# A second batch of filler matmuls behind the last y of unit 0, stages and loads at new positions

## The chip, the cores and the metric

One core of one Trainium2 chip runs the whole program in one launch. The metric is the device time of that core in microseconds (us), less is better; the time before is the median of three runs. A further execution was taken by the hardware profiler, and all rows below come from it.

## The reference

The reference has two parts, one behind the other.

```python
# q, k, v, a_re, a_im: (4, 8, 768, 48) float32
mag = sqrt(a_re**2 + a_im**2)
scale = minimum(mag, 0.999) / (mag + 1e-6)
for t in range(768):                      # a complex state S of 48 x 48 per batch and head
    S = (a_re + 1j*a_im)[t][:, None] * scale[t][:, None] * S + k[t] (outer) v[t]
    y[t] = q[t] @ real(S)
x = y.transpose(0, 2, 1, 3).reshape(3072, 384)
# w_in: (384, 2048), w_out: (2048, 384), drawn as float64
h = x @ w_in
g = h * tanh(softplus(h))                 # softplus(h) = h above 20
out = (g @ w_out).astype(float32)
```

## The kernel before, in words

The 3072 rows are cut into 12 units of 256 time steps (three per batch), a unit into two chunks of 128 steps. Each unit goes through three stages.

1. `ew_steps(u)`, elementwise. Loads of a_re and a_im (tiles R and I, L247), q and k (QK, L255) and v (V, L262). ScalarE (ACT) takes squares, logarithms and exponentials (L123); VectorE (DVE) sums the log magnitudes along time (the scan at L333), ACT takes two exponentials of the sum and GpSimd (POOL) multiplies q and k with them (L375, unit 0 on DVE). The angles go the same way: an arctangent on ACT (L143), a second scan (L347), the reduction to one turn (L352, L353), sines on ACT (L143; each way into and out of this group costs a table load, L131), and the products with q and k (`rot`, L397: the X products with t=0 of a unit 1 or 2 chunk on POOL, the others on DVE). DMAs on SyncE's (SP's) queue relay the products into the tile T (L388), in which rows are the 96 inner positions of a head. For units 0 and 1 the chunks are handled one by one, later units in one piece.
2. `attn_steps(u)`, attention by chunks on TensorE (PE). `kn` transposes k (L459, copied by ACT at L460), `amat` takes k times q (pa, L467; masked into am by DVE at L470), `upd` takes the new part of the state (pd, L497) that DVE adds and scales (L501, L503, L505; from unit 1 on L505 is POOL's), `yv` sums y in PSUM (L483), and ACT copies it out (L488). `fin` relays y into the layout of x by four DMAs (xf, L516) and splits it into a high and a low part, xH by ACT (L157) and xL by DVE (L158), three column groups each.
3. `moe_steps`, the two dense layers. `mm1(j)` takes x times the j-th of eight pairs of column groups of w_in, 18 matmuls into ph (L543) in three products (xH·wiH, xL·wiH, xH·wiL); ACT and DVE make g of it (L547 to L553, split into gh and gl at L556); `mm2(j)` multiplies with w_out into po (L571).

The weights come as 64-bit numbers. `convert` makes 12 chunks of w_in (raw) and 12 of w_out (wraw) into a high and a low 32-bit part: ACT turns the low word (L123), DVE shifts the high word (L190, L194), POOL adds the two (L199), then a cast gives wiH or wo (L157, two of three on ACT, one on DVE) and DVE takes the rest (wiL or wo, L158). All of it stands between the start of the program and the last of the first dense layers, beside the elementwise work of units 0 to 3.

The order is set by numbers. Each step has a place in a plan (EW for elementwise, AT for attention, LD for loads, WP for weights, FIN0 for unit 0's `fin`, WK for the filler) and a shift of its rank (ES, TS, WS, MB); `tile_kernel` sorts the steps by place to write them and by shifted place to give them a priority, and a scheduler at build time fixes from priorities and dependencies the order of each engine's instructions. Every engine then runs its list in order, and waits where the head of it waits. SP issues the DMAs in list order too.

The filler is `warm` (L428): 18 matmuls of bf16 with 512 columns into a PSUM tile that nobody reads, which wait by a hand-made dependency for unit 0's first reduced angle (L353).

Of the kernel before, what the change touches and what calls it, by code (L numbers as in the profile page):

```python
# [41 lines left out]
GACT = 0  # L42
GATE = -1
GRP = 2
RG, QG, GN = 5, 1, 0
SQ0, SORD, CGA, CGN, CGD, ACTG = 1, 0, 3, 3, 0, 0
YDVE = []
RQ = [(), ()]
LG, WG = -1, 12
W1 = 0  # L50
ADDV = 12
CLAMPP, MAGP = 0, 0
# [1 line left out]
ROTP = [2]  # L54
TREE = 1
WXB, WRB, WI = 1, 2, 512
FIN0 = -3.39
FS = 0.0
TRUNC = 0
AFTERX = 0  # L60
NUN = 12
SUBP = 0
MULP = 1
LONG = 2
WIDE = 1
NWARM, WREP, WK = 2, 9, -9.4
FAST = [0, 1]
EW = [(-16.31, -10.95), (-12.73, -8.83), (-13.6, -11.78), (-17.21, -10.84), (-16.32, -10.6)]
AT = [(-7.75, -4.28), (-4.18, -0.81), (-7.43, -2.2), (-9.42, -3.06), (-10.26, -2.73)]
WP = [(-7.98, -3.45), (-3.03, 2.5), (2.11, 8.49), (9.4, 9.68)]  # L70
WS = [-3.58, -0.64, -1.09, 0.24]
ES = [2.49, -0.99, -0.86, 1.6]
TS = [-0.14, -1.22, 2.46, -0.05]
MB = [-1.35, -0.11]
WL1 = -1.83
RB = 2
XB = 2
LD = [(-17.86, -16.7, -16.5), (-19.19, -20.26, -20.22), (-17.97, -17.71, -17.6), (-21.41, -14.83, -16.39), (-24.18, -15.85, -17.38)]
WL = 512
XRUNS = ((0, 0, 0, 32), (0, 1, 32, 16), (64, 1, 64, 16), (0, 2, 80, 32))  # L80
LOW, HIGH, FADED = 0.55, 2e6, 1e-17
# [5 lines left out]
def tile_kernel(ctx, tc, q, k, v, are, aim, w_in, w_out, out):  # L87
    nc = tc.nc
# [78 lines left out]
    turned = []  # L167
# [4 lines left out]
    def load_win(half):  # L172
        def f():
            for o in range(0, NJ * DF // 2, WL):
                ins = nc.sync.dma_start(raw_in[half][:, o:o + WL],
                                        w_in[:, half * NJ * DF // 2 + o:half * NJ * DF // 2 + o + WL])
                if half:
                    after(ins, placed[3] if o // WL >= RG else qloads[-1] if QG else relayed[-1])
        return f
# [50 lines left out]
    def ew_steps(u):  # L230
# [45 lines left out]
        def get(g):  # L276
            return (*(flat(st[n], g) for n in ("R", "I", "X1")), *(part(st["X"][:, :, :, a], g) for a in range(2)))
# [26 lines left out]
        def slope(g):  # L304
            R, I, X1, x2, x3 = get(g)
            (nc.gpsimd if 0 < u <= MULP else nc.vector).tensor_tensor(I, I, X1, ALU.mult)
            (nc.gpsimd if 0 < u <= CLAMPP else nc.vector).tensor_scalar(I, I, -1.5, 1.5, ALU.max, ALU.min)
# [129 lines left out]

    def attn_steps(u):
        b, uu = divmod(u, NU)
        st = units[u]  # L440
# [6 lines left out]
        def chunk(c):  # L447
            first = uu == 0 and c == 0
            last = uu == NU - 1 and c == NCH - 1
            cs = slice(c * C, (c + 1) * C)  # L450
# [23 lines left out]
            def yv(g):  # L474
                def f():
                    py = ypsum
                    for i in (2 * g, 2 * g + 1):
                        for n, old in enumerate(((True, False), (False, True))[u < WIDE] if not first else (False,)):
                            for par in range(2):
                                h = 2 * i + par  # L480
                                lhs = d["S"][:, h, :] if old else st["V"][:, c, h * D:(h + 1) * D]
                                rhs = st["T"][c][:, h, 0, :C] if old else d["am", h // 4][:, h % 4, :]
                                nc.tensor.matmul(py[64 * par:64 * par + D, i, :], lhs, rhs,  # L483
                                                 start=n == 0, stop=first or n == 1)
                    if g == 1:
                        if c == 0:
                            st["y"] = at.tile([112, 4, TU], F32, tag="y", name="y", bufs=1)
                        (nc.vector.tensor_copy if u < 1 and c in YDVE else nc.scalar.copy)(st["y"][:, :, cs], py)  # L488
                return f

            def upd():
# [100 lines left out]
    plan = []  # L592

    def place(steps, first, last, shift=0.0):
        n = len(steps)
        for i, f in enumerate(steps):
            x = first + (last - first) * i / max(n - 1, 1)
            plan.append((x, len(plan), f, x + shift))
# [3 lines left out]
    for u in range(NUN):  # L602
        slot = slots.get(u, range(NPAIR * u, NPAIR * (u + 1)))
        t0 = slot[0]
        place(ew_steps(u), t0 + EW[min(u, len(EW) - 1)][0], t0 + EW[min(u, len(EW) - 1)][1], ES[min(u, 3)])
        for n, f in enumerate(units[u]["load"]):
            x = t0 + LD[min(u, len(LD) - 1)][n]
            plan.append((x, len(plan), f, x))
        asteps = attn_steps(u)
        if u == 0:  # L610
            plan.append((FIN0, len(plan), asteps.pop(), FIN0 + FS))
        place(asteps, t0 + AT[min(u, len(AT) - 1)][0], t0 + AT[min(u, len(AT) - 1)][1], TS[min(u, 3)])
        moe = moe_steps(units[u], u * TU, u, u < 2)
        for j in range(NPAIR):
            plan.append((slot[j], len(plan), moe[0][j], slot[j] + MB[0]))
            plan.append((slot[j] + LAG + 0.5, len(plan), moe[1][j], slot[j] + LAG + 0.5 + MB[1]))
    plan.append((-15.9, len(plan), load_win(0)))
    plan.append((WL1, len(plan), load_win(1)))
    if NWARM:
        plan.append((WK, len(plan), warm))  # L620
    n = HALF // WI
    for i, f in enumerate((win, wout)):
        for half in range(2):
            place([f(n * half + m) for m in range(n)], *WP[2 * half + i], WS[2 * half + i])
    rank = {x[:2]: i for i, x in enumerate(sorted(plan, key=lambda x: (x[3] if len(x) > 3 else x[0], x[1])))}
# [22 lines left out]
def general(tc, nc, q, k, v, are, aim, pools, moe_steps, split):  # L648
    io, ew, at, ps, dram = (pools[n] for n in ("io", "ew", "at", "ps", "dram"))
    BJ = B * NJ  # L650
    TS = 8
    xs = dram.tile([B, S, DM], F32, name="xs")
# [14 lines left out]
    kv, t1, t2, t3, t4 = w1[:, 0], w1[:, 1], w2[:, 0], w2[:, 1], w3  # L667
    n = B * TS * D
    m = BJ * TS
    big = at.tile([P, n + 5 * m], F32, tag="T", name="big", bufs=TB)  # L670
    more = at.tile([P, 3 * m + BJ * D], F32, tag="T", name="more", bufs=TB)
    vb = big[:, 0:n].rearrange("p (b t e) -> p b t e", b=B, t=TS)
    cols = [x[:, o + i * m:o + (i + 1) * m].rearrange("p (b j t) -> p b j t", b=B, j=NJ)
            for x, o, cnt in ((big, n, 5), (more, 0, 3)) for i in range(cnt)]
    cq, ck, cr, ci, cm, ca, cb, cc = cols
    qs = more[:, 3 * m:].rearrange("p (a e) -> p a e", e=D)
    ysb = at.tile([H, B, TS, D], F32, tag="T", name="ysb", bufs=TB)
    tt, ts = nc.vector.tensor_tensor, nc.vector.tensor_scalar
# [132 lines left out]
```

## Time and profile before

| | us |
|---|---|
| median of three runs | 655.73 |
| the three runs | 652.61, 655.73, 659.77 |
| the profiled execution's own time | 653.54 |
| its span in the trace | 651.7 |

The span begins with the first instruction of the trace and ends with the last; the 1.8 us around it are the launch. In the profile's rows PE, PEld, DVE, ACT and POOL are TensorE's matmuls and weight loads, VectorE, ScalarE and GpSimd, SPq is the DMA queue of SyncE. A timeline row gives start, length, engine, line, operation, the tiles written and read, and in brackets the idle time before it with what ended it. The granted clock is TensorE's, as a share of 2.4 GHz: 1.00 is the upper of its two levels, 0.50 the lower, 1.2 GHz.

### The profile page before, as it was taken

The page shows a single profiled execution, that of the slowest core. Times are in us where ns is not written, and L with a number is a line of the kernel's source. Part 1 is how long each engine was busy: PE and PEld are TensorE (multiplying, and loading weights), DVE is VectorE, ACT ScalarE, POOL GpSimd, SP SyncE. Part 2 cuts the span into 40 slices and gives each one's busy share as a digit, 9 for nine tenths or more (in the row PEclk, how much of TensorE's full clock was granted, in tenths as well). Part 3 has the DMA queues.
Part 4 walks back from the last instruction along what each step waited for, and adds up shares of the span by engine and source line. Part 5 has one row for each costly group of instructions (what it writes and reads, how often), then busy time and mean ns, then how long its engine had stood idle before and what let it go on. Part 6 is the DMA issues. An engine that isn't in the chain of part 4 may idle for free.

```text
span 651.7 us, 11747 instructions
## 1 busy us (share of the span) xinstructions
PE 581.7 (89%) x4468; PEld 554.5 (85%) x4468; DVE 502.1 (77%) x875; ACT 489.2 (75%) x785; POOL 127.5 (20%) x101
## 2 busy tenths in 40 slices
PE   0686956698689999999999999999999999999996
PEld 0475846598579999999989999999899999999995
DVE  6968989999848869878869868978788796544552
ACT  7857967797757778887988977977888878645661
POOL 2316257435201112002003003003012030000000
PEclk9856888599779999999999999999999999999999
DMA  8765723612840270260460530621711602201000
GB/s 303 219 238 142 245 82 101 190 33 85 210 144 13 87 191 5 89 179 1 117 153 25 143 101 26 183 63 29 192 49 49 171 2 83 64 26 25 1 26 29
DMA packets 58528, 67.05 MB, mean 103 GB/s; under 512 B 4960, under 2 KB 51040, under 8 KB 58464
## 3 DMA queue, kind: packets, MB, share of 16 engines
q1 hardware_dynamic: 58464, 66.23, 35.1%
q8 instruction: 37, 0.61, 0.4%
q14 instruction: 27, 0.22, 0.1%
HBM read 36.96 MB, written 5.51 MB: 65 GB/s over the span
## 4 chain that ended last, share of the span: by engine, by line
PE 38%; DVE 23%; ACT 18%; DMA 7%; issue 7%; SPq 5%; POOL 2%; DVEq 0%; POOLq 0%; ACTq 0%
PE ph L543 14%; PE po L571 13%; ACT e L123 6%; ACT L131 4%; PE pa L467 4%; PE ypsum L483 4%; DVE e L548 3%; DMA R<-a_re 3%; ACT X L123 3%; SPq L388 3%; DVE gl L158 3%; DMA T<-QK 3%; DVE X L347 2%; PE pd L497 2%; DVE R L333 2%
## 5 line engine op out<-in xcount | busy, mean ns | idle before, releaser
L571 PE MATMUL po<-wo,gh 128*128 128x384 f32 x768 | 221.0, 348 | 16.8 <-DVE wo L157 6.0
L543 PE MATMUL ph<-xH,wiH 128*128 128x256 f32 x576 | 169.3, 295 | 10.4 <-ACT xH L157 9.6
L543 PE MATMUL ph<-xL,wiH 128*128 128x256 f32 x576 | 167.3, 291 | 3.1 <-DVE xL L158 3.1
L543 PE MATMUL ph<-xH,wiL 128*128 128x256 f32 x576 | 167.7, 291 | 0.9 <-DVE wiL L158 0.9
L571 PEld LDWEIGHTS po<-wo,gh 128*128 128x128 f32 x768 | 141.6, 190 | 22.5 <-DVE wo L157 6.7
L123 ACT ACTIVATE e<-e 128x512 f32<-128x512 f32 x192 | 119.7, 629 | 50.8 <-DVE e L548 48.9
L571 PE MATMUL po<-wo,gl 128*128 128x384 f32 x384 | 131.3, 342 | 0.0
L543 PEld LDWEIGHTS ph<-xH,wiH 128*128 128x128 f32 x576 | 113.4, 197 | 14.4 <-ACT xH L157 10.4
L543 PEld LDWEIGHTS ph<-xL,wiH 128*128 128x128 f32 x576 | 113.4, 197 | 4.1 <-DVE xL L158 4.1
L543 PEld LDWEIGHTS ph<-xH,wiL 128*128 128x128 f32 x576 | 113.5, 197 | 1.1 <-DVE wiL L158 1.1
L505 POOL TENSOR_TENSOR S<-S,T 96x384 f32<-96x384 f32 x18 | 27.6, 1533 | 314.7 <-DVE S L503 110.3
L553 DVE SCALAR_TENSOR_TENSOR g<-e,ph 128x512 f32<-128x512 f32 x96 | 65.3, 680 | 22.2 <-ACT e L123 21.3
L548 DVE TENSOR_SCALAR e<-e 128x512 f32<-128x512 f32 x96 | 55.9, 583 | 31.5 <-ACT e L123 31.3
L158 DVE TENSOR_TENSOR gl<-g,gh 128x512 fp32r<-128x512 f32 x96 | 75.0, 781 | 1.6
L123 ACT ACTIVATE e<-ph 128x512 f32<-128x512 f32 x96 | 56.5, 591 | 24.6 <-PE ph L543 24.4
L571 PEld LDWEIGHTS po<-wo,gl 128*128 128x128 f32 x384 | 73.1, 190 | 0.4 <-issue 0.4
L123 ACT ACTIVATE e<-e,fifth 128x512 f32<-128x512 f32 x96 | 69.1, 720 | 1.8
L157 DVE CAST gh<-g 128x512 fp32r<-128x512 f32 x96 | 41.0, 427 | 34.3 <-PE po L571 32.6
L131 ACT ACT_TABLE_LOAD x45 | 57.7, 1283 | 1.6 <-PEq L767 0.8
L375 POOL TENSOR_TENSOR QK<-QK,X 128x1536 f32<-128x1536 f32 (+1 forms) x12 | 40.5, 3377 | 76.8 <-ACT X L123 73.2
L467 PE MATMUL pa<-T 96*128 96x128 f32 x384 | 52.9, 288 | 0.6 <-DVE am L470 0.6
L467 PEld LDWEIGHTS pa<-T 96*128 96x128 f32 x384 | 49.5, 203 | 1.2 <-DVE am L470 0.8
(89 smaller groups left out, 820.8 us busy)
## 6 DMA issues: line engine op xcount, KB each, us to landing
T<-X SPq DMA_DIRECT2D x72, 129.0 KB, 2.5
T<-QK SPq DMA_DIRECT2D x72, 129.0 KB, 3.3
raw<-w_in SPq DMA_DIRECT2D x12, 512.0 KB, 9.2
wraw<-w_out SPq DMA_DIRECT2D x12, 512.0 KB, 4.4
QK<-q SPq DMA_DIRECT2D x12, 384.0 KB, 4.3
QK<-k SPq DMA_DIRECT2D x12, 384.0 KB, 5.1
V<-v SPq DMA_DIRECT2D x12, 384.0 KB, 4.6
out_dram<-o SPq DMA_DIRECT2D x24, 192.0 KB, 1.9
```

What stands on the lines that cost most here:

```text
L123: ins = nc.scalar.activation(out, in_, func, **kw)
L131: ins = nc.scalar.preload_act_table_set(name)
L157: heng(h, src)
L158: leng(out=lo, in0=src, in1=h.bitcast(F32), op=ALU.subtract)
L375: (nc.vector if g in FAST and u == 0 else nc.gpsimd).tensor_tensor(QK[..., :C], QK[..., :C], X[..., :C], ALU.mult)
L467: nc.tensor.matmul(pa[:, i, :], st["T"][c][:, 4 * g + i, 1, :C], st["T"][c][:, 4 * g + i, 0, :C], start=True, stop=True)
L483: nc.tensor.matmul(py[64 * par:64 * par + D, i, :], lhs, rhs, start=n == 0, stop=first or n == 1)
L505: (nc.vector if u < WIDE else nc.gpsimd).tensor_tensor(nS, nS, pe, ALU.mult)
L543: nc.tensor.matmul(ph[:, a, :], wi[wp][:, j, kt, a * P:a * P + P], st[xp][:, kt, :], start=n == 0, stop=n == 8)
L548: nc.vector.tensor_scalar_min(e, e, math.exp(20.0))
L553: nc.vector.scalar_tensor_tensor(g, e, 2.5, ph, ALU.subtract, ALU.mult)
L571: nc.tensor.matmul(po[t], gp[:, a, tsl], wo[part][:, wp, 2 * i + a, :], start=j in starts and a == 0 and n == 0, stop=j + 1 in ends and a ...
```

## The change

`warm` becomes `spin`, which is placed twice: 18 filler matmuls as before (into one tile in place of two times 9 into two), and 12 more that wait for ACT's second copy of y in unit 0 (L488, chunk 1). All the places and shifts of units 0, 1, 2 and 3 move. Three switches change: MULP = 0 gives unit 1's products of angle and inverse magnitude (L306) to DVE, where POOL had them; LG = 12 frees the loads of unit 2's R, I and V from a wait for unit 1's last relay; RG = 3 puts three in place of one of w_in's second six loads behind unit 0's xf DMAs.

```diff
-RG, QG, GN = 5, 1, 0
+RG, QG, GN = 3, 1, 0
-LG, WG = -1, 12
+LG, WG = 12, 12
-FIN0 = -3.39
+FIN0 = -2.63
-MULP = 1
+MULP = 0
-NWARM, WREP, WK = 2, 9, -9.4
+WREP, WREP2, WK = 18, 12, -8.6
-EW = [(-16.31, -10.95), (-12.73, -8.83), (-13.6, -11.78), (-17.21, -10.84), (-16.32, -10.6)]
+EW = [(-16.11, -10.98), (-12.73, -8.83), (-13.6, -11.78), (-17.88, -11.79), (-16.43, -10.6)]
-ES = [2.49, -0.99, -0.86, 1.6]
+ES = [3.85, -0.77, -2.02, 1.25]
...
-    def warm():
-        for i in range(NWARM):
+    copied = []
+
+    def spin(count, prev):
+        def f():
             junk = ps.tile([P, 512], F32, tag="po", name="junk", bufs=2)
-            for _ in range(WREP):
+            for _ in range(count):
                 ins = nc.tensor.matmul(junk, cmask, cmask.unsqueeze(1).broadcast_to([P, 4, P]), start=True, stop=True)
-                tc.add_manual_dep(ins.ins, turned[0].ins.name,
+                tc.add_manual_dep(ins.ins, prev[0].ins.name,
                                   mybir.DependencyInfo(mybir.DependencyClass.Sync, mybir.DependencyReason.DATA), reason="clock")
+        return f
...
-                        (nc.vector.tensor_copy if u < 1 and c in YDVE else nc.scalar.copy)(st["y"][:, :, cs], py)
+                        ins = (nc.vector.tensor_copy if u < 1 and c in YDVE else nc.scalar.copy)(st["y"][:, :, cs], py)
+                        if u == 0 and c == 1:
+                            copied.append(ins)
...
-    if NWARM:
-        plan.append((WK, len(plan), warm))
+    plan.append((WK, len(plan), spin(WREP, turned)))
+    if WREP2:
+        plan.append((FIN0 + 0.01, len(plan), spin(WREP2, copied)))
```

AT, WP, WS, TS, MB, WL1 and LD change in the same way as EW and ES. On PE the 12 new matmuls stand between unit 0's last y matmul (L483) and its first ph matmul (L543). In the lists below the lines of the changed kernel are its own: L463 is before's L460, L473 is L470, L491 is L488, L508 is L503, L510 is L505.

DVE, around the end of unit 0's attention (am, S and pd are unit 0's chunk 1; R, I and QK are unit 1's), before:

```order
L470 TENSOR_TENSOR am<-pa,cmask 128x512
L503 TENSOR_TENSOR S<-pd,S 96x192 x2
L333 SCALAR_TENSOR_TENSOR R<-rmask,R 128x384
L329 SCALAR_TENSOR_TENSOR R<-X 128x384
L505 TENSOR_TENSOR S<-S,T 96x384
L333 SCALAR_TENSOR_TENSOR R<-rmask,R 128x384
L381 TENSOR_SCALAR cnt,good<-QK 128x3
L346 SCALAR_TENSOR_TENSOR I<-ncar,I 128x3
L347 SCALAR_TENSOR_TENSOR X_234<-rmask,I 128x384
```

The same place in the changed kernel:

```order
L329 SCALAR_TENSOR_TENSOR R<-X 128x384
L333 SCALAR_TENSOR_TENSOR R<-rmask,R 128x384
L510 TENSOR_TENSOR S<-S,T 96x384
L333 SCALAR_TENSOR_TENSOR R<-rmask,R 128x384
L473 TENSOR_TENSOR am<-pa,cmask 128x512
L508 TENSOR_TENSOR S<-pd,S 96x192 x2
L510 TENSOR_TENSOR S<-S,T 96x384
L381 TENSOR_SCALAR cnt,good<-QK 128x3
L346 SCALAR_TENSOR_TENSOR I<-ncar,I 128x3
L347 SCALAR_TENSOR_TENSOR X_214<-rmask,I 128x384
```

Both of unit 1's scans of log magnitudes (L333) moved from behind the state update that waits for pd to ahead of it.

ACT, unit 1's arctangents and sines with unit 0's last copy of y and its xH casts, before:

```order
L488 COPY y<-ypsum 112x4x128
L123 ACTIVATE raw_99<-raw_99 128x512
L123 ACTIVATE X<-R 128x3x128 x2
L131 ACT_TABLE_LOAD
L143 ACTIVATE I<-I 128x384 x2
L123 ACTIVATE raw_99<-raw_99 128x512 x3
L157 CAST xH<-xf 128x256 x3
L143 ACTIVATE X_234<-I 128x384
L143 ACTIVATE R<-I 128x384
```

The same place in the changed kernel:

```order
L131 ACT_TABLE_LOAD
L143 ACTIVATE I<-I 128x384 x2
L123 ACTIVATE raw_99<-raw_99 128x512
L491 COPY y<-ypsum 112x4x128
L143 ACTIVATE X_214<-I 128x384
L143 ACTIVATE R<-I 128x384
L157 CAST xH<-xf 128x256
L143 ACTIVATE R<-R,halfpi 128x384
L143 ACTIVATE X_214<-I 128x384
L143 ACTIVATE R<-I 128x384
L157 CAST xH<-xf 128x256
```

The copy of y moved behind the arctangents, and the three xH casts, which stood ahead of all sines, are spread among them; the third follows the table load behind the sines.

POOL, the adds of w_out's chunks (wraw) and the scalings of unit 1's state (S), before:

```order
L199 TENSOR_TENSOR wraw_497<-wraw_497 128x512
L505 TENSOR_TENSOR S_642<-S_642,T_389 96x384
L199 TENSOR_TENSOR wraw_517<-wraw_517 128x512
L505 TENSOR_TENSOR S_774<-S_774,T_414 96x384
L199 TENSOR_TENSOR wraw_577<-wraw_577 128x512
L375 TENSOR_TENSOR QK_512<-QK_512,X_731 128x12x128
```

The same place in the changed kernel:

```order
L199 TENSOR_TENSOR wraw_509<-wraw_509 128x512
L510 TENSOR_TENSOR S_663<-S_663,T_395 96x384
L199 TENSOR_TENSOR wraw_529<-wraw_529 128x512
L199 TENSOR_TENSOR wraw_576<-wraw_576 128x512
L510 TENSOR_TENSOR S_824<-S_824,T_413 96x384
L199 TENSOR_TENSOR wraw_654<-wraw_654 128x512
L375 TENSOR_TENSOR QK_518<-QK_518,X_743 128x12x128
```

The add of the fourth w_out chunk (wraw_577, now wraw_576) moved from behind the second scaling of the state to ahead of it, the fifth's (wraw_654) from behind unit 2's L375 to ahead of it.

## Rows read from the trace of the kernel before

**Rows 1.** The page, the span in 40 slices of 16.3 us: PE, DVE, data moved.

```profile
PE   0686956698689999999999999999999999999996
DVE  6968989999848869878869868978788796544552
...
GB/s 303 219 238 142 245 82 101 190 33 85 210 144 13 87 191 5 89 179 1 117 153 25 143 101 26 183 63 29 192 49 49 171 2 83 64 26 25 1 26 29
```

**Rows 2.** Busy time by stretches: stretch, length, five engines, granted clock, DMA share, GB/s.

```profile
28.00:46.00 18.00, 18.00 (x119) 16.84 (x119) 13.85 (x28) 8.77 (x18) 4.09 (x4) 0.53 0.81 275
46.00:49.00 3.00, 0.63 (x10) 0.37 (x6) 0.56 (x3) 2.30 (x5) 2.54 (x4) 0.97 0.10 14
50.00:59.00 9.00, 5.61 (x24) 5.31 (x25) 8.40 (x21) 8.21 (x16) 5.51 (x5) 0.50 0.37 95
...
64.00:70.00 6.00, 6.00 (x32) 5.42 (x32) 6.00 (x10) 4.84 (x9) 2.34 (x3) 0.50 0.90 274
70.00:90.00 20.00, 18.05 (x169) 16.03 (x169) 20.00 (x40) 18.67 (x29) 5.80 (x4) 1.00 0.51 160
90.00:96.00 6.00, 0.34 (x2) 0.03 (x1) 3.86 (x5) 0.41 (x1) 5.56 (x2) 0.83 0.39 122
96.00:121.00 25.00, 14.53 (x70) 12.89 (x70) 23.97 (x34) 18.61 (x29) 14.09 (x9) 0.70 0.30 85
...
200.00:640.00 440.00, 436.19 (x3517) 423.52 (x3516) 332.32 (x570) 341.68 (x538) 52.16 (x39) 1.00 0.28 78
```

**Rows 3.** Timeline, single rows that carry durations of moved or added work.

```profile
8.49 0.55 DVE L306 TENSOR_TENSOR I<-I,X 128x384 f32<-128x384 f32 x1
...
17.68 6.31 PE L432 MATMUL junk<-cmask 128*128 128x512 bf16 x18 [17.68 <-DVE I L353]
...
21.17 1.86 DVE L397 TENSOR_TENSOR QK<-QK,R 128x384 f32<-128x384 f32 x2
...
71.36 0.84 ACT L123 ACTIVATE X<-R 128x768 f32<-128x768 f32 x1
```

**Rows 4.** Timeline, the end of unit 0's attention and unit 1's angles, 43 to 64 us.

```profile
43.39 0.35 DVE L503 TENSOR_TENSOR S<-pd,S 96x192 f32<-96x192 f32 x1 [0.93 <-PE pd L497]
43.66 0.95 DVE L333 TENSOR_TENSOR_SCAN R<-rmask,R 128x384 f32<-128x384 uint8 x1
...
45.45 0.95 DVE L333 TENSOR_TENSOR_SCAN R<-rmask,R 128x384 f32<-128x384 uint8 x1
...
46.68 0.58 ACT L488 COPY y<-ypsum 112x512 f32<-112x512 f32 x1 [1.10 <-PE ypsum L483]
...
52.89 0.80 PE L543 MATMUL ph<-xH,wiH 128*128 128x256 f32 x2 [6.26 <-ACT xH L157]
53.00 0.53 DVE L353 SCALAR_TENSOR_TENSOR I<-X,I 128x384 f32<-128x384 f32 x1
...
54.29 5.75 POOL L397 TENSOR_TENSOR X<-QK,X 128x384 f32<-128x384 f32 x2 [3.49 <-ACT X L143]
...
60.01 1.04 POOL L199 TENSOR_TENSOR raw<-raw 128x512 int32<-128x512 int32 x1
...
61.08 0.66 ACT L157 CAST wiH<-raw 128x512 fp32r<-128x512 f32 x1 [2.65 <-POOL raw L199]
...
62.45 0.68 DVE L158 TENSOR_TENSOR wiL<-raw,wiH 128x512 fp32r<-128x512 f32 x1
```

**Rows 5.** The tile xf, its DMAs from issue to landing, 40 to 110 us.

```profile
DMA to landing us min/median/max: 2.4/2.7/4.3
```

**Rows 6.** Timeline, a scaling of the state on POOL and what waits behind it.

```profile
78.84 1.49 POOL L505 TENSOR_TENSOR S<-S,T 96x384 f32<-96x384 f32 x1 [6.44 <-DVE S L503]
...
87.76 6.80 POOL L505 TENSOR_TENSOR S<-S,T 96x384 f32<-96x384 f32 x1 [3.35 <-DVE S L503]
...
94.53 1.03 POOL L199 TENSOR_TENSOR wraw<-wraw 128x512 int32<-128x512 int32 x1
...
96.29 0.69 PE L571 MATMUL po<-wo,gh 128*128 128x384 f32 x1 [5.95 <-ACT wo L157]
```

More of the change, by code (lines that the diff above doesn't have):

```diff
@@ L62 @@
 SUBP = 0
-MULP = 1
+MULP = 0
 LONG = 2
 WIDE = 1
-NWARM, WREP, WK = 2, 9, -9.4
+WREP, WREP2, WK = 18, 12, -8.6
 FAST = [0, 1]
-EW = [(-16.31, -10.95), (-12.73, -8.83), (-13.6, -11.78), (-17.21, -10.84), (-16.32, -10.6)]
-AT = [(-7.75, -4.28), (-4.18, -0.81), (-7.43, -2.2), (-9.42, -3.06), (-10.26, -2.73)]
-WP = [(-7.98, -3.45), (-3.03, 2.5), (2.11, 8.49), (9.4, 9.68)]
-WS = [-3.58, -0.64, -1.09, 0.24]
-ES = [2.49, -0.99, -0.86, 1.6]
-TS = [-0.14, -1.22, 2.46, -0.05]
-MB = [-1.35, -0.11]
-WL1 = -1.83
+EW = [(-16.11, -10.98), (-12.73, -8.83), (-13.6, -11.78), (-17.88, -11.79), (-16.43, -10.6)]
+AT = [(-7.62, -4.55), (-3.79, -0.81), (-8.05, -2.82), (-8.41, -3.06), (-10.49, -2.73)]
+WP = [(-7.98, -3.4), (-2.82, 2.46), (1.94, 7.2), (9.3, 9.35)]
+WS = [-3.58, -1.77, 0.11, 1.02]
+ES = [3.85, -0.77, -2.02, 1.25]
+TS = [0.08, -1.31, 2.46, -0.05]
+MB = [-1.35, -0.14]
+WL1 = -0.98
 RB = 2
 XB = 2
-LD = [(-17.86, -16.7, -16.5), (-19.19, -20.26, -20.22), (-17.97, -17.71, -17.6), (-21.41, -14.83, -16.39), (-24.18, -15.85, -17.38)]
+LD = [(-17.86, -17.24, -16.49), (-18.78, -19.85, -19.81), (-17.97, -17.71, -17.6), (-21.23, -15.07, -17.56), (-24.18, -15.85, -17.38)]
 WL = 512
```

## The prediction

> **What bounds the kernel now.** I read the page's slices first: PE is full from the thirteenth slice, some 200 us, to the end, and before that it has holes, while DVE is high [rows 1]. The stretches say it in numbers: from 200 to 640 us PE is busy 436.19 of 440.00 us, so the steady part has 3.8 us to win at most; from 70 to 90 and from 96 to 121 us DVE is busy 20.00 of 20.00 and 23.97 of 25.00, and PE 14.53 of the latter [rows 2]. The start is therefore set first by PE (28 to 46 us, 18.00 of 18.00, at a granted clock of 0.53), then by hand-offs between all engines, and from about 60 us by DVE, which makes w_in, w_out, unit 1's and unit 2's angles and the dense layers' g all at once. DVE has one large hole before that: 18.00 − 13.85 = 4.2 us between 28 and 46 us and 2.4 us between 46 and 49 us [rows 2]. Third, the timeline from 43 to 64 us shows the chain that fills this gap late: unit 1's scans stand behind the state update that waits for pd, ended by PE at 43.39; only then come exponentials, arctangents, angles (L353 at 53.00), the products on POOL (54.29, two in 5.75 us), the add of w_in's fourth chunk behind them on POOL (60.01), its cast (61.08) and its rest wiL (62.45 to 63.13), which the third ph waits for [rows 4]. Fourth, a scaling of the state holds POOL for 6.80 us, and PE waits 5.95 us for the chunk of w_out behind it [rows 6].
>
> **The change part by part.** The sum is made on the profiled execution: 653.54 us of its own, span 651.7 us and 1.8 us around it. The median shown is 655.73, or 2.2 us above.
>
> *Step 1, unit 0 up to its last y.* In the new lists DVE makes the QK products of chunk 0 ahead of a weight chunk's L194, which can save 1 us of the 1.86 us pair beside the wait [rows 3]; against it ACT takes two squares of unit 2 (0.84 us each [rows 3]) ahead of a wiH cast and of unit 0's copies of k, and DVE takes the two L306 that POOL had (MULP, 0.55 us each [rows 3]) ahead of am. Counted row by row I get the last y copied at about 46.9 instead of 47.26 us, which is nothing; the ends are −1.0 and +1.7 us (both squares on the path). The loads of R and I of unit 2 come 0.79 MB earlier, in front of unit 0's relays on SP. The first slice moved 303 GB/s and the second 219 [rows 1], a room of 84 GB/s times 16.3 us, 1.4 MB: I cost them at nothing, and at 0.79 MB through 303 GB/s, +2.6 us, if that cover is gone.
>
> *Step 2, unit 1's scans.* With both L333 ahead of the S update, the angles no longer wait for scans, exponentials and a table load behind 43.39 us. What is late next is the S update itself (43.39 + 0.35 and a scaling that I take at L306's 0.55, so 44.3 us). Behind it come the count, two scans of 0.95 and the short rows that before filled the 2.5 us from 50.5 us to 53.00, with a wait for POOL's QK pieces of about 0.9 us in between: L353 at about 47.7 in place of 53.00 us [rows 4], 5.3 us earlier. DVE does this in its hole, and the 1.1 us of the two L306 as well, so these cost nothing; without the hole they cost 1.1 us.
>
> *Step 3, sines, POOL products, w_in.* On ACT, in order, the copy of y (46.9), two of the first chunk's sines' rows, then the first xH cast. It waits for the first of the four xf DMAs: issued at 47, it lands 2.7 us later [rows 5], with SP's 0.6 us of issue 50.3 us. Behind it a sine (0.6) and the second chunk's sine (0.5): 51.8 us, where POOL's second product can start. It takes half of 5.75 us [rows 4], so the add of w_in's fourth chunk runs from 54.7 to 55.7. ACT has a table load, the third xH cast, one row of unit 2 and one weight row in front of the wiH cast, which ends at 57.3, and DVE's wiL ends at 58.0 us in place of 63.13 us [rows 4]: −5.1 us. DVE has by then done the same rows as before at 63.13, and two L306 more, so DVE is 5.1 us ahead.
>
> *Step 4, the second filler.* 18 filler matmuls took 6.31 us [rows 3]; with one level twice as fast as the other that is about 11.5 of them at 0.43 us and 6.5 at 0.21 us, so 12 take 5.1 us at the lower level of the clock and half of it at the upper one. They start behind the copy of y, at 46.9, when the granted clock is already 0.97 [rows 2], so they end at 49.5 us, and at 52.0 us if it falls. PE has nothing in this time: ph waited 6.26 us for xH [rows 4], and with xH's third cast at 55 us it still waits. Cost 0; if the cover went, 52.0 − 50.7 = +1.3 us. Gain in the sum: 0 as well. The clock was 0.50 from 50 to 59 us, after PE had been idle for those 6.26 us [rows 2, 4], so ph may now run at the upper level, but what follows it waits for wiH and wiL. The bound below: half of PE's 5.61 us in this stretch and half of its 6.00 us from 64 to 70 us, also at 0.50 [rows 2], −5.8 us.
>
> *Step 5, POOL's order.* The add that stood behind the 6.80 us scaling now stands ahead of it, so PE's 5.95 us wait for it goes [rows 6]. Since DVE is the bound on both sides of it, only DVE's own idle time there counts: 6.00 − 3.86 = 2.1 us [rows 2]. The next piece behind the scaling is a chunk of w_out that is due later. I take −2.1 us; the ends are 0 (the scaling just delays the next chunk) and −5.95 us.
>
> Here a rule of the skill speaks against the change. The two scalings on POOL took 1.49 and 6.80 us for the same tile [rows 6]; the long one lies beside a DVE that ran nearly without gaps. The Trainium skill, SBUF — State Buffer, section "Who interferes with whom", says that a DVE instruction with two SBUF inputs and a GpSimd one that reads SBUF exclude each other, and that the later one waits for the whole of the other. The 6.80 us agree with it. By it a DVE that is filled in 28 to 60 us would hold POOL up just there; what this does is the last rival below, and the sum by it would be above the time before.
>
> *Step 6, the rest.* From 96 to 200 us the same rows follow in nearly the same order, so DVE's lead is carried along, and the waits for relays and xf between 168 and 187 us move with it. From 200 us on PE is full [rows 2] and its work is the same but for the filler, so the lead comes out at the end. I cost this at 0, with ±2 us for the transfers that meet at other places.
>
> The sum is −5.1 − 2.1 = −7.2 us: 653.54 − 7.2 = 646.3 us on the profiled execution's scale. The median of before is 2.2 us above that scale; with a third of it, 647.0 us, 1.3% below 655.73.
>
> **The rivals.** A change under 1% (6.6 us) is about what a measurement of this kernel can't tell from none.
>
> *The xH casts hold the sines up.* ACT runs in order, and a cast that waits for xf now keeps unit 1's second sines behind it. Before, the first cast ended only at 52.85, just ahead of ph at 52.89 [rows 4]. For it: a load of V for unit 2 now stands ahead of xf on SP. Against it: the queue moved only 14 GB/s from 46 to 49 us [rows 2]. If the first cast comes at 52.4 instead of 50.3, all of step 3 is 2.1 us later, DVE's lead is 3.0 us, and with step 5 lost against the later POOL the time is 653.54 − 3.0 = 650.5, on the median's scale 651.5 us.
>
> *The clock gives back more.* If the filler keeps the clock at 1.00 until the dense layers run, and PE and not DVE sets the pace from 63 to 70 us, the 5.8 us of step 4 come on top of the forecast: 647.0 − 5.8 = 641.2 us. For it: the clock is 0.97 when the filler starts, and PE is busy 6.00 of 6.00 us from 64 to 70 us [rows 2]. Against it: DVE is also busy 6.00 of 6.00 there [rows 2], and PE's work from 50 to 57 us will come in drips, as the xH casts do. The Trainium skill, TensorE: Matmul & The Clock Gate, section "Why this matters for your kernels", advises to leave no idle gaps between bursts of matmuls, since the clock goes back after them; the drop to 0.50 behind the 6.26 us agrees.
>
> *The filler does not do what it is for.* If the clock falls all the same, the forecast stays: it contains nothing of the clock.
>
> *POOL is starved, and the kernel is slower.* One mechanism: DVE, now without holes from 38 us on, stretches POOL's pieces as the scaling was stretched, from 1.49 to 6.80 us [rows 6]. The place is the pair of products ahead of the fourth chunk of w_in: at 6.80 us each from 48.2 us they end at 61.8 instead of 60.04 us, +1.8 us; the same stretch on the moved scaling puts 5.3 us in front of the fifth chunk of w_out, so nothing of step 5 is won: +7.1 us, 655.73 + 7.1 = 662.8 us. It decides from the point where the fourth chunk's add on POOL ends later than the 61.05 us of before [rows 4]. Against it: L306 on POOL goes away, and the products were already at 2.9 us each.
>
> **How the numbers follow.** Forecast 0.45, xH casts 0.26, clock 0.16, starved POOL 0.13. Faster by over 1% is a time below 649.2: 0.85 of the forecast's cases, all of the clock's and 0.15 of the first rival's, 0.38 + 0.16 + 0.04 = 0.58. Slower by over 1% is above 662.3: half of the last rival's cases and some outliers of others, 0.09. The rest, 0.33, is within. The range reaches from under the clock's case (641.2 less the 2 us of step 6) to the lower edge of the slower one: 639 to 658 us.
>
> **What would show it.** Right: L353 of unit 1 near 48 us; the POOL add of w_in's fourth chunk before 57 us; wiL of it near 58 us; no wait of 5 us of po for wo around 85 to 95 us; the same density of PE behind 200 us, reached some 7 us earlier. Step 1 is wrong if the last copy of y comes after 48.5 us. Step 4 is wrong if the first ph waits for the filler and not for xH. The forecast is wrong if DVE is ahead at 58 us but PE's dense part starts no earlier, or if DVE's idle time before 60 us is as large as before.

## The result, and the profile after

| | before | after |
|---|---|---|
| median, us | 654.91 (of 4 runs) | 647.51 (of 4 runs) |
| runs, us | 652.61 to 659.77 | 646.57 to 647.86 |
| profiled execution, us | 653.54 | 647.57 |
| its span, us | 651.7 | 645.8 |

A fourth run of the kernel before was made beside those of the changed one. The ratio of the times is 0.9866, with a 95% interval of 0.982 to 0.9912: about 1.3% faster, where 647.0 us (639 to 658) had been forecast. Between the profiled executions it is 6.0 us. The sum came out, but two of its terms did not, and the traces show where.

The page of the changed kernel in 40 slices of 16.1 us (PE, DVE, data moved), against [rows 1]:

```profile
PE   0698975888699989999999999999999999999996
DVE  6989899899769869859868867977788796644551
...
GB/s 301 264 184 247 162 115 106 176 38 75 239 103 25 119 154 1 130 141 13 134 125 25 173 75 26 197 50 53 192 28 70 152 5 101 46 25 26 1 26 29
```

The second slice moves 264 GB/s in place of 219: unit 2's loads do come earlier. The third, fourth, sixth and eighth slice of PE are fuller, the seventh and ninth a tenth emptier; PE is full from the twelfth on but for the fifteenth, where it was full from the thirteenth on before.

Stretches of [rows 2], and one more from 0 to 64 us (columns: stretch, length, busy us of PE, weight load, DVE, ACT, POOL with the number of instructions, then granted clock, DMA share, GB/s):

```profile
46.00:49.00 3.00, 2.31 (x21) 1.77 (x18) 2.86 (x11) 0.81 (x2) 0.66 (x3) 0.50 0.16 18
64.00:70.00 6.00, 6.00 (x61) 5.37 (x59) 5.77 (x10) 5.80 (x11) 2.19 (x2) 1.00 0.92 299
90.00:96.00 6.00, 4.20 (x16) 3.08 (x16) 6.00 (x10) 5.24 (x9) 1.49 (x2) 0.56 0.31 96
200.00:640.00 440.00, 436.33 (x3504) 423.29 (x3498) 324.95 (x562) 340.19 (x534) 50.28 (x39) 1.00 0.28 77
0.00:64.00 64.00, 39.06 (x201) 29.72 (x202) 55.49 (x113) 47.44 (x90) 19.87 (x32) 0.76 0.81 248
```

The hole of DVE is closed: 46 to 49 us holds 2.86 us of work, where [rows 2] had 0.56. Up to 64 us DVE has been busy 55.49 us. The same line of the kernel before:

```profile
0.00:64.00 64.00, 34.31 (x188) 28.11 (x188) 49.80 (x105) 44.44 (x85) 23.46 (x33) 0.78 0.70 226
```

So DVE has been busy 55.49 − 49.80 = 5.7 us longer at 64 us. That is not yet work done: 1.1 us of it are the two L306 that POOL had, and a row that runs beside one of POOL can take longer (L510 below 1.51 us, where 0.55 is usual). So I also counted the rows that DVE had done by a date, each at the median length of its kind over the fourteen traces of this case, less the 1.1 us where DVE has those two L306. Counted in this way DVE is 4.2 us ahead at 64 us and 3.1 us at 165 us. From 200 us on nothing changed (436.33 against 436.19 of 440 us).

The timeline from 39 to 62 us, against [rows 4] (start, length, engine, line, operation, tiles, and in brackets the idle time before it):

```profile
39.10 0.95 DVE L333 TENSOR_TENSOR_SCAN R<-rmask,R 128x384 f32<-128x384 uint8 x1
40.41 0.95 DVE L333 TENSOR_TENSOR_SCAN R<-rmask,R 128x384 f32<-128x384 uint8 x1
44.54 0.35 DVE L508 TENSOR_TENSOR S<-pd,S 96x192 f32<-96x192 f32 x1 [0.93 <-PE pd L502]
44.92 1.51 DVE L510 TENSOR_TENSOR S<-S,T 96x384 f32<-96x384 f32 x1
48.13 0.59 ACT L491 COPY y<-ypsum 112x512 f32<-112x512 f32 x1 [1.91 <-PE ypsum L486]
48.77 4.94 PE L434 MATMUL junk<-cmask 128*128 128x512 bf16 x12 [0.69 <-ACT y L491]
48.98 0.53 DVE L353 SCALAR_TENSOR_TENSOR I<-X,I 128x384 f32<-128x384 f32 x1
50.22 0.97 POOL L397 TENSOR_TENSOR X<-QK,X 128x384 f32<-128x384 f32 x1 [3.56 <-ACT X L143]
52.02 0.41 ACT L157 CAST xH<-xf 128x256 fp32r<-128x256 f32 x1 [1.53 <-DMA xf<-y]
53.36 0.59 PE L548 MATMUL ph<-xH,wiH 128*128 128x256 f32 x2
53.50 1.34 POOL L397 TENSOR_TENSOR X<-QK,X 128x384 f32<-128x384 f32 x1 [2.31 <-ACT X L143]
54.80 1.35 POOL L199 TENSOR_TENSOR raw<-raw 128x512 int32<-128x512 int32 x1
56.82 0.58 PE L548 MATMUL ph<-xL,wiH 128*128 128x256 f32 x1 [2.17 <-DVE xL L158]
60.61 0.68 DVE L158 TENSOR_TENSOR wiL<-raw,wiH 128x512 fp32r<-128x512 f32 x1
```

Both scans are done before pd is; L353 comes at 48.98 in place of 53.00 us; the last y is copied at 48.72; the add of w_in's fourth chunk ends at 56.15 in place of 61.05 us, and its wiL at 61.29 in place of 63.13 us.

POOL's scalings and adds of w_out, two rows of DVE beside them, and PE's wait, against [rows 6]:

```profile
73.09 3.94 POOL L510 TENSOR_TENSOR S<-S,T 96x384 f32<-96x384 f32 x1
84.05 3.03 POOL L199 TENSOR_TENSOR wraw<-wraw 128x512 int32<-128x512 int32 x1 [4.30 <-ACT wraw L123]
86.13 1.38 DVE L328 TENSOR_SCALAR X<-X 128x768 f32<-128x768 f32 x1
87.05 1.15 POOL L510 TENSOR_TENSOR S<-S,T 96x384 f32<-96x384 f32 x1
87.42 1.06 DVE L553 TENSOR_SCALAR e<-e 128x512 f32<-128x512 f32 x1
89.75 0.44 PE L576 MATMUL po<-wo,gh 128*128 128x384 f32 x1 [2.85 <-ACT wo L157]
```

The second scaling takes 1.15 in place of 6.80 us, and the wait of 5.95 us is 2.85.

To see what became of the lead I counted PE's matmuls in both traces, each kind weighted by its time at the upper clock (0.12 us for ph, 0.18 for po), and compared the times at which the same amount was done. The changed kernel is 2.6 us ahead at 71 us, 6.4 at 98, 5.5 at 146, then 0.0 at 149 and −0.4 at 183, and 6.3 at 194, which stays to the end. So PE's lead is lost and won again. DVE's counted lead is still 3.1 us at 165 us, though it is as low as 0.4 us at 149 us, and −2.0 us at 174 us. PE's is lost here, where a g comes late on DVE:

```profile
145.93 0.58 PE L548 MATMUL ph<-xH,wiH 128*128 128x256 f32 x1 [3.45 <-DVE g L558]
```

It is won where unit 2's x is relayed for the dense layers. Before:

```profile
175.10 1.51 PE L459 MATMUL pkn<-ident,T 96*128 96x96 f32 x8 [6.44 <-DMA T<-QK]
180.01 4.55 SPq L516 DMA_DIRECT2D xf<-y  x4
186.58 0.40 ACT L157 CAST xH<-xf 128x256 fp32r<-128x256 f32 x1 [5.44 <-DMA xf<-y]
187.04 0.58 PE L543 MATMUL ph<-xH,wiH 128*128 128x256 f32 x1 [2.90 <-ACT xH L157]
```

And after:

```profile
173.48 1.51 PE L462 MATMUL pkn<-ident,T 96*128 96x96 f32 x8 [5.94 <-DMA T<-QK]
175.53 2.57 SPq L521 DMA_DIRECT2D xf<-y  x4
178.14 0.60 SPq L255 DMA_DIRECT2D QK<-k  x1
181.38 0.70 ACT L157 CAST xH<-xf 128x256 fp32r<-128x256 f32 x2
```

Before, unit 2's last y matmuls stood behind unit 3's transposes of k (pkn), which wait 6.44 us for relays; now they stand ahead of them, xf is issued 4.5 us earlier, ahead of the load of k, and ph does not wait. The prediction says of this place only that its waits move with the lead. That the change of places wins the time is not shown: e6 below undoes it and loses nothing.

### The profile page after: what moved, and what is told of

It is laid out like the page before. It is cut to its first block, busy times and chain, and to the rows that moved or that the text cites. A ratio compares the mean times of both kernels' runs of the same rounds, so it can differ in the third digit from the quotient of the medians.

```text
span 645.8 us, 11762 instructions
## 1 busy us (share of the span) xinstructions
PE 583.5 (90%) x4480; PEld 554.0 (86%) x4480; DVE 500.8 (78%) x877; ACT 490.7 (76%) x785; POOL 119.9 (19%) x99
## 4 chain that ended last, share of the span: by engine, by line
PE 68%; DVE 12%; DMA 7%; issue 4%; POOL 3%; ACT 3%; SPq 2%; POOLq 0%; DVEq 0%
PE po L576 26%; PE ph L548 24%; PE pa L470 6%; PE ypsum L486 6%; PE pd L502 3%; DMA T<-QK 2%; PE pkn L462 2%; DVE wx L190 1%; DMA raw<-w_in 1%; POOL raw L199 1%; DMA R<-a_re 1%; DMA wraw<-w_out 1%; ACT e L123 1%; DVE e L553 1%; SPq L388 1%
## 5 line engine op out<-in xcount | busy, mean ns | idle before, releaser
L553 DVE TENSOR_SCALAR e<-e 128x512 f32<-128x512 f32 x96 | 58.1, 605 | 32.9 <-ACT e L123 32.7
L510 POOL TENSOR_TENSOR S<-S,T 96x384 f32<-96x384 f32 x18 | 23.0, 1279 | 266.4 <-DVE S L508 113.9
L158 DVE TENSOR_TENSOR gl<-g,gh 128x512 fp32r<-128x512 f32 x96 | 70.8, 737 | 1.6
L375 POOL TENSOR_TENSOR QK<-QK,X 128x1536 f32<-128x1536 f32 (+1 forms) x12 | 40.2, 3353 | 103.2 <-ACT X L123 90.7
L470 PE MATMUL pa<-T 96*128 96x128 f32 x384 | 52.0, 287 | 0.0
L470 PEld LDWEIGHTS pa<-T 96*128 96x128 f32 x384 | 48.9, 201 | 0.9 <-issue 0.7
```

The lines of the kernel that those rows point to most:

```text
L158: leng(out=lo, in0=src, in1=h.bitcast(F32), op=ALU.subtract)
L375: (nc.vector if g in FAST and u == 0 else nc.gpsimd).tensor_tensor(QK[..., :C], QK[..., :C], X[..., :C], ALU.mult)
L470: nc.tensor.matmul(pa[:, i, :], st["T"][c][:, 4 * g + i, 1, :C], st["T"][c][:, 4 * g + i, 0, :C], start=True, stop=True)
L510: (nc.vector if u < WIDE else nc.gpsimd).tensor_tensor(nS, nS, pe, ALU.mult)
L553: nc.vector.tensor_scalar_min(e, e, math.exp(20.0))
```

## The experiments

Twelve kernels ran; each ratio is to the kernel before, run on the same chip. The list scheduler orders what stands behind an edit anew, so each expectation says up to where the lists agree.

**The filler's size** (labels e1 to e4):

```diff
-WREP, WREP2, WK = 18, 12, -8.6
+WREP, WREP2, WK = 18, 0, -8.6
```

and 4, 8 and 20 in place of 0.

> The changed kernel without the second filler (0 in place of 12 matmuls). All engines keep their lists up to about the 107th instruction of DVE (some 65 us); behind that the scheduler, which counts the filler's time, gives another order. Theory A (the filler's matmuls are worth nothing in themselves, the order of the lists is all): first ph at about 52.4 in place of 53.4 us, the same rows at 61 to 65 us within 0.5 us of the changed kernel, and a time set by the other list alone, 645 to 651 us. Theory B (the clock is the gain): granted clock 0.50 from 50 to 70 us as before, the rows at 61 to 65 us at least 2 us later, time 650.5 us or more.

> The changed kernel with 4 matmuls in the second filler; all lists but for the filler are those of the kernel with none. Theory A: within 0.7 us of the kernel with no second filler. Theory B: between that one and the changed kernel, 0.7 to 2 us under the one with none.

> The changed kernel with 8 matmuls in the second filler; all lists but for the filler are those of the changed kernel. Theory A: filler ends near 52.2 us, first ph at 52.4 behind the cast of xH, time within 0.7 us of 647.5. Theory B: the clock stays at 0.50 up to 70 us and about 3 us are lost (half of the 6 us from 64 to 70 us), 650.5 us.

> The changed kernel with 20 matmuls in the second filler; all lists but for the filler are those of the changed kernel. Theory A: 8 more at 0.21 us each from 53.6 us, first ph near 55.3 us, mostly hidden since ph waits for xL until 56.8 us in the changed kernel: 647.5 to 648.5 us. Theory B: the clock is 1.00 without a break from 53 us to 70 us, time under 646.5 us.

Measured: 0.9882 (0.9836 to 0.9927) with none, 0.9886 (0.9851 to 0.992) with 4, 0.9882 (0.9822 to 0.9942) with 8, 0.9879 (0.983 to 0.9927) with 20, beside 0.9866 with 12. All five are one time. In microseconds e3 (644.80) and e4 (645.22) came out under what theory A named, and e4 where theory B wanted it; but the kernel before was faster beside them too (653.83 in place of 654.91 us), and e1 with no filler took 645.82. Without the filler:

```profile
52.90 0.80 PE L548 MATMUL ph<-xH,wiH 128*128 128x256 f32 x2 [4.57 <-ACT xH L157]
...
64.00:70.00 6.00, 5.15 (x54) 4.80 (x50) 6.00 (x12) 4.64 (x10) 2.83 (x2) 1.00 0.97 320
```

The clock is 1.00 from 64 to 70 us without any filler, where it was 0.50 before [rows 2], and DVE is full (6.00 of 6.00) all the same. Theory B falls: the filler's matmuls win nothing. What the clock itself is worth there these runs do not say, since it was 1.00 in all five; it is not enough, since it was 1.00 there in e5, e9 and e10 below too.

**Unit 2's last y on PE** (e5, e6). In e5 unit 3's first transposes are made to follow unit 2's last y matmul, in the kernel before; in e6 the last 12 y matmuls follow the transposes, in the changed kernel.

```diff
+                        if u == 3 and c == 0:
+                            after(ins, lasty[2])
```

> The kernel before with one edit: unit 3's first transposes of k (pkn) must follow unit 2's last y matmuls on PE, which stood behind them. 6 matmuls change places, every other list is that of the kernel before. Theory C (the forecast's: DVE's lead of the early stages is carried to the end): no early stage is touched, so at most 1 us is won. Theory D (the early leads are used up by 180 us, and what is left at the end is made between 168 and 194 us, where unit 2's last y comes ahead of the transposes, so that xf is relayed sooner): y copied some 8 us earlier, no wait of ph for xH near 187 us, 4 to 7 us faster than the kernel before.

> The changed kernel with the opposite edit: unit 2's last 12 y matmuls must follow unit 3's first transposes of k. All lists are those of the changed kernel up to about 165 us; behind that the scheduler's order changes with it (on SP the xf DMAs again follow V and both QK loads). Theory C: the leads of the early stages stay, 6 to 8 us faster than the kernel before. Theory D: the wait of ph for xH near 187 us is back, within 2 us of the kernel before.

e5: 0.9946 (0.9921 to 0.9971), 3.5 us faster; e6: 0.9882 (0.9841 to 0.9922), no slower than the changed kernel beyond the intervals. In e5 neither theory holds: C allowed 1 us, D wanted 4 to 7. In e6 theory C's forecast came true (6 to 8 us; 0.9882 is 7.7 us) and theory D's failed. In e5 the mechanism was not the expected one either: y is not copied earlier, since the copy has its old place on ACT's list, and xf is as late as before:

```profile
177.56 1.51 PE L460 MATMUL pkn<-ident,T 96*128 96x96 f32 x8 [2.06 <-DMA T<-QK]
179.54 0.56 ACT L491 COPY y<-ypsum 112x512 f32<-112x512 f32 x1
180.93 2.58 SPq L519 DMA_DIRECT2D xf<-y  x4
...
165.00:195.00 30.00, 24.15 (x163) 22.12 (x162) 22.91 (x43) 22.12 (x38) 3.80 (x3) 0.83 0.69 193
```

PE is busy 24.15 of the 30 us from 165 to 195, where the kernel before was 20.31: the wait for T shrank from 6.44 to 2.06 us, and the one for xH is gone. In e6 the last y stands behind the transposes again and xf behind both loads of QK, but all of it is early:

```profile
169.96 1.51 PE L463 MATMUL pkn<-ident,T 96*128 96x96 f32 x8 [4.22 <-DMA T<-QK]
174.25 0.59 ACT L495 COPY y<-ypsum 112x512 f32<-112x512 f32 x1 [0.30 <-PE ypsum L490]
```

The relays that the transposes wait for have landed by 169.96 us, where it was 175.10 us before, and xH is ready at 180.99 us. PE's lead grows from 1.4 us at 183 to 7.8 us at 194 us, much as in the changed kernel. So the change of places is not needed to win the time back.

**POOL's order** (e7 in the kernel before, e8 in the changed one): the scaling of unit 1's chunk 1 follows the add of w_out's fourth chunk, or the reverse. In e7 unit 2's last y is held behind unit 3's transposes, so that nothing of e5 comes in.

```diff
+                if n == 3 and "S" in adds:
+                    after(adds["S"], ins)
```

> The kernel before with POOL's add of w_out's fourth chunk ahead of the second scaling of unit 1's state, and unit 2's last y matmuls held behind unit 3's transposes, where they were. The lists are those of the kernel before up to about 85 us; behind that the scheduler's order differs in detail. Both theories: no wait of po of 5.95 us near 90 us, PE's work 4 to 6 us ahead at 98 us. Theory C: it stays, 4 to 6 us faster than the kernel before. Theory D: it is used up by 180 us, between 2 us faster and 1 us slower.

> The changed kernel with POOL's add of w_out's fourth chunk behind the second scaling of unit 1's state, as it was before. The lists are those of the changed kernel up to about 80 us; unit 2's last y still stands ahead of unit 3's transposes. Both theories: the wait of po near 90 us is back, 5 to 6 us. Theory C: these are lost at the end, 1 to 4 us faster than the kernel before. Theory D: nothing is lost, 6 to 9 us faster than the kernel before.

e7: 1.003 (1.0007 to 1.0053), 2 us slower, just beyond theory D's 1 us; the wait of 5.95 us is gone, and PE's work is 3.9 us ahead at 98 us, 1.6 behind at 125. Its DVE is 1.5 us behind by count at 64 us already, where its lists are still those of before, so this much is the scatter of single executions. e8: 0.9866 (0.9816 to 0.9916), as fast as the changed kernel:

```profile
84.07 5.67 POOL L515 TENSOR_TENSOR S<-S,T 96x384 f32<-96x384 f32 x1 [5.07 <-DVE S L513]
91.47 0.69 PE L585 MATMUL po<-wo,gh 128*128 128x384 f32 x1 [1.66 <-ACT wo L157]
```

The scaling is long again, but po waits 1.66 us, not the 5 to 6 that both theories gave, so e8 does not test what that wait is worth. What POOL's order is worth at the end rests on e7: nothing. There theory C falls, and of D it holds that such a lead is used up.

**Unit 1's scans** (e9 and e10 in the kernel before, e11 in the changed one). e9 puts both scans ahead of the update of unit 0's chunk 1 state on DVE, and the copy of its y behind unit 1's exponentials on ACT; e10 has the first alone:

```diff
+    for x in marks["S", 0, 1]:
+        for y in marks["scan", 1, 0] + marks["scan", 1, 1]:
+            after(x, y)
+    for x in marks["y", 0, 1]:
+        for y in marks["exp", 1, 1]:
+            after(x, y)
```

In e11 the scans follow the state update, and unit 1's arctangents on ACT follow the copy of y:

```diff
+    for x in marks["scan", 1, 0] + marks["scan", 1, 1]:
+        for y in marks["S", 0, 1]:
+            after(x, y)
+    for x in marks["atan", 1, 0]:
+        for y in marks["y", 0, 1]:
+            after(x, y)
```

> The kernel before with step 2 alone: unit 1's two scans (L333) ahead of unit 0's state update on DVE, and unit 0's second copy of y behind unit 1's exponentials on ACT (the arctangents come ahead of it too). No filler, no change of loads, MULP as before. The lists are those of the kernel before up to there; behind it the scheduler's order differs, and unit 2's last y comes ahead of unit 3's transposes. Theory E (DVE's empty time from 45 to 50 us is what the change fills, and work done early on DVE is carried): last reduced angle (L353) 3 to 5 us earlier, DVE 3 to 6 us more busy than before by 64 us, 6 to 9 us faster than the kernel before. Theory F (only what stands behind 165 us decides): as with the y matmuls alone, 3 to 4 us faster.

> As the last one, but on DVE alone: the scans ahead of the state update, while on ACT unit 0's second copy of y stays ahead of unit 1's second exponentials, the table load and the arctangents. Theory E: the angles still wait for the copy of y, L353 within 1.5 us of before's 53.0 us, DVE's work by 64 us within 2 us of before, so 2 to 5 us faster than the kernel before (the share of the y matmuls), and 3 us or more slower than with ACT's order too. Theory F: the same time as with ACT's order too, within 1.5 us.

> The changed kernel with step 2 undone: unit 1's scans behind unit 0's state update, the arctangents behind the second copy of y. The lists are those of the changed kernel up to there; the second filler, loads and L306 stay as changed; behind it the order differs, unit 2's last y still stands ahead of unit 3's transposes. Theory E: L353 back to 52 to 54 us, DVE's work by 64 us at most 2 us above before, 3 to 6 us slower than the changed kernel. Theory F: within 1.5 us of the changed kernel.

e11: 0.9946 (0.991 to 0.9983), that is 0.8% or some 5 us slower than the changed kernel, though the two intervals just touch:

```profile
45.38 1.79 DVE L342 TENSOR_TENSOR_SCAN R<-rmask,R 128x384 f32<-128x384 uint8 x2
53.73 0.53 DVE L362 SCALAR_TENSOR_TENSOR I<-X,I 128x384 f32<-128x384 f32 x1
...
0.00:64.00 64.00, 34.31 (x196) 25.19 (x196) 50.14 (x107) 47.27 (x90) 18.88 (x31) 0.84 0.77 243
```

L353 (L362 here) is back at 53.73 us, and DVE's lead at 64 us is 50.14 − 49.80 = 0.3 us. By count it is −0.1 us. So theory E holds in the changed kernel, with two reserves: behind the edit the lists are in another order, and the granted clock from 64 to 70 us was 0.50 in this trace, as before. The lead was gone by 60 us, ahead of that stretch. e9: 0.9968 (0.9937 to 0.9998), 2.1 us faster; e10: 1.0028 (1.0006 to 1.0051), 1.8 us slower. They are 3.9 us apart, as E said and F did not, but not in E's way: L353 comes at 51.17 and 51.78 us. Nor does e9 have E's lead:

```profile
43.75 0.96 DVE L342 TENSOR_TENSOR_SCAN R<-rmask,R 128x384 f32<-128x384 uint8 x1
51.17 0.53 DVE L362 SCALAR_TENSOR_TENSOR I<-X,I 128x384 f32<-128x384 f32 x1
...
0.00:64.00 64.00, 33.51 (x181) 27.31 (x182) 54.60 (x108) 44.65 (x85) 20.51 (x34) 0.76 0.70 228
```

The order is that of the changed kernel, but the second scan starts at 43.75 us, where the changed kernel has it at 40.41, and L353 is 1.8 us earlier in place of 3 to 5. DVE has been busy 54.60 − 49.80 = 4.8 us longer by 64 us (3.9 in e10), but with 108 rows, where before has 105 and the changed kernel 113: its rows took longer. By count e9 is 1.6 and e10 1.2 us ahead at 64 us, which is no more than the scatter above, and 2.4 and 2.7 behind at 165 us. So the two do not test whether the lead is enough. Late in e9:

```profile
179.91 1.51 PE L469 MATMUL pkn<-ident,T 96*128 96x96 f32 x8 [5.15 <-DMA T<-QK]
183.40 1.57 SPq L264 DMA_DIRECT2D QK<-k  x1
185.01 1.94 SPq L527 DMA_DIRECT2D xf<-y  x3
189.66 0.71 ACT L166 CAST xH<-xf 128x256 fp32r<-128x256 f32 x2 [1.96 <-DMA xf<-y]
```

In e9's list three of the four xf DMAs stand behind both QK loads, and xH is complete at 190.37 us, later than before (188.69).

**Unit 3's transposes later** (e12, in the changed kernel). Its first transposes stand behind 22 matmuls of the dense layers:

```diff
+                        if u == 3 and c == 0:
+                            after(ins, mms[1, 6])
```

> The changed kernel with unit 3's first transposes of k behind 22 matmuls of the dense layers on PE, which stood behind them; every other list is unchanged. PE waited 5.94 us for the relays there. If those matmuls are ready, PE does up to 3 us of work in the wait, 1 to 3 us faster than the changed kernel; if the po among them wait for w_out's cast themselves, nothing is won, within 1 us.

It came to 0.986 (0.9833 to 0.9886), the changed kernel's time. The second case of the expectation holds; the wait only changes its name:

```profile
172.18 0.69 PE L579 MATMUL po<-wo,gh 128*128 128x384 f32 x1 [5.28 <-ACT wo L157]
```

All runs side by side; "busy" is DVE's busy time up to 64 us less the 49.80 of before, "counted" its lead in rows done as above, xH the end of unit 2's last xH cast, all in us:

| kernel | ratio | busy, 64 | counted, 64 | counted, 165 | xH |
|---|---|---|---|---|---|
| before | 1 | 0 | 0 | 0 | 188.69 |
| after | 0.9866 | 5.7 | 4.2 | 3.1 | 182.08 |
| e1: no filler | 0.9882 | 5.5 | 3.7 | 4.1 | 174.86 |
| e2: 4 fillers | 0.9886 | 4.4 | 2.9 | 3.8 | 173.94 |
| e3: 8 fillers | 0.9882 | 5.7 | 4.3 | 3.6 | 181.26 |
| e4: 20 fillers | 0.9879 | 4.4 | 2.7 | 4.6 | 180.17 |
| e6: after, y last | 0.9882 | 5.5 | 4.0 | 4.7 | 180.99 |
| e8: after, POOL's order of before | 0.9866 | 6.0 | 4.5 | 4.2 | 177.22 |
| e12: after, k later | 0.986 | 4.4 | 2.7 | 3.8 | 178.72 |
| e11: after, scans late | 0.9946 | 0.3 | −0.1 | −2.4 | 182.16 |
| e5: before, y first | 0.9946 | 1.7 | 0.3 | −2.6 | 188.41 |
| e9: before, scans early | 0.9968 | 4.8 | 1.6 | −2.4 | 190.37 |
| e10: before, scans early on DVE alone | 1.0028 | 3.9 | 1.2 | −2.7 | 190.21 |
| e7: before, POOL's order of after | 1.003 | −1.9 | −1.5 | −3.6 | 192.18 |

The eight kernels with a counted lead of 2.7 us or more at 64 us all have 3 us or more at 165 us and are 1.1 to 1.4% faster. The other five, with 1.6 us or less, stand 2.4 to 3.6 us behind at 165 us and lie between 0.5% faster and 0.3% slower. (The trace of before is of one of its faster executions, 653.54 us, which may be why all five stand behind it.) An xH at 182 us without the lead is not enough: e11 keeps 0.5%. The lead with a late xH no run has, and an xH 7 to 8 us earlier still (e1, e2) adds nothing. The gap between the two groups at 64 us is within the scatter of single executions, the one at 165 us is not. That DVE's lead is the cause fits all rows, and e11, which takes step 2 back, shows it for some 5 us of the change's 8 to 9. What the remaining 0.5% comes from is open, and no run gave the kernel before the lead.

## Why the prediction was right, point by point

Total: forecast −7.2 us on the profiled execution, measured −6.0; the median came 0.5 us from the forecast.

- Step 1 (nothing, −1.0 to +1.7): the last y is copied at 48.72 us, 1.46 later than before, and by the prediction's own mark (48.5) the step is wrong, though inside its bounds. 0.61 us are there at the first transpose, 28.16 in place of 27.55 us, although the relays to it were issued 1.0 us earlier (22.08 in place of 23.07): they took longer beside the earlier loads (a median of 4.2 us from issue to landing, in place of 2.5), so the room for these was not quite free. The rest I did not trace.
- Step 2 (L353 5.3 us earlier): right, 4.0 us. Two things that came later make up for the difference: the second half of pd's update starts at 44.54 in place of 43.39 us, and the scaling L510 took 1.51 us where I took 0.55.
- Step 3 (DVE 5.1 us ahead): right in size (4.2 us by count), wrong in its marker. wiL came only 1.8 us earlier, since DVE did rows of later stages ahead of it; the sentence that it "has by then done the same rows as before" failed. e11 shows that steps 2 and 3 are needed, at some 5 us; whether they are enough no run shows, since e9 did not bring the lead about.
- Step 4 (filler nothing): right (e1 to e4). By its mark it was wrong: the first ph waited for the filler, which ended at 53.7 us at a clock of 0.55, while xH was there at 52.43. It cost nothing, because ph then waited 2.17 us for xL.
- Step 5 (POOL's order −2.1 us): wrong, it is the lower end of its range, 0. What failed is that DVE's idle time there would be won. In e7 DVE is busy through more of it (1.9 us behind in busy time at 64 us, 0.4 ahead at 98), but mostly with rows that took longer: by count it goes from 1.5 us behind to 1.1 behind, and PE's lead is gone at 125 us. The scaling behind the add took 7.47 us in e7, which fits the prediction's own case for 0, that it delays the next chunk.
- Step 6 (the rest as before, 0 ± 2): within its bounds as a sum, from 4.2 us at 64 us to 6.0 at the end, and right that DVE's lead is carried, 3.1 us at 165 us. On PE it is not: 5.5 us go at 146 to 149 us, and 6.7 come back from 183 to 194 us, a loss and a gain that I did not foresee. "The waits for relays and xf between 168 and 187 us move with it" failed: the transposes start only 1.6 us earlier (173.48 in place of 175.10), and the wait for xH went away. Why it went away is open, since e6 has none either with y, xf and the transposes in the places of before.
- The rivals: the first xH cast came at 52.02 us, close to the 52.4 of "xH casts hold the sines up", yet the add on POOL ended at 56.15, 0.5 us behind my forecast. By the third of 2.2 us that the forecast takes, this rival's time is 651.3 and not 651.5 us. The clock was 1.00 from 64 to 70 us, as "the clock gives back more" had it, and PE did 61 matmuls there in place of 32, but the time is 6 us above that case's; DVE was busy 5.77 of the 6.00 us, and the clock rose without the filler too. POOL was not starved: its two products took 0.97 and 1.34 us, in place of 5.75 for both.

So the total owes something to luck: steps 2 and 3 carry it, step 5's 2.1 us were not there, and about as much came in later stages, from a place that no run here settles.

## What to carry to other kernels

A lead on a busy engine is not read from one marker row, because a scheduler may put other rows ahead of the marker, nor from busy time alone, because rows that take longer count as busy too: e9 was 4.8 us ahead in busy time and 1.6 in rows done. Count the rows done by a date. Follow the lead to the last place where the full engine waits, and look at more than one engine: PE's lead was nothing at 149 us while its work still came out 6 us earlier at the end. An early transfer late in the start-up is not enough by itself: e11 had xH as early as the changed kernel and kept 0.5% of 1.3%. A removed wait on an engine that is not the bound (PE's 5.95 us) is worth what the next stage can take up, which in e7 was nothing.

## What the runs showed of the hardware

- The granted clock rises at different times in executions of the same instructions. From 46 to 49 us, in a stretch that is mostly y matmuls, one upon the other, it was 0.50 in the changed kernel, 0.64 in e1 and 0.67 in e4; the 12 filler matmuls took 4.94 us at 0.55, and in e4 20 took 4.49 us at 1.00.
- DVE and POOL make each other's rows longer. The same scaling on POOL takes 0.84 to 7.47 us (e7). At 3.94 us (73.09) the row beside it is mostly L158, with two tensor inputs, at its usual length; at 1.15 us (87.05) it is DVE's rows with one input that take longer, L328 1.38 us (0.55 at 88.62 in the kernel before) and L553 1.06 us (0.42 at 74.71). The Trainium skill, SBUF — State Buffer, section "Who interferes with whom", says that a DVE instruction with two SBUF inputs contends with a GpSimd instruction that reads SBUF, and that `tensor_scalar`, as L328 and L553 are, can contend as well; these rows agree. The 6.80 us of [rows 6] and the 6.87 and 7.47 us of e11 and e7 lie beside scans, among others.
- In the fourteen traces 529 rows of DVE are over 0.3 us longer than the median of their kind, and every one of them overlaps a row of POOL; of all rows of DVE 20% do. This is why DVE's busy time ran ahead of its work in e9.
- Matmuls that compute nothing change the program through the scheduler: with 0 to 4 of them all other lists are one order, with 8 to 20 another, from about 65 us on.
